# Both halves of an expert tile's first layer issued ahead of the two relus

## The chip, the core and the metric

The kernel runs on one core of one Trainium2 chip. The metric is the device time of one execution in microseconds (us). PE (TensorE) multiplies, DVE (VectorE) and ACT (ScalarE) read its results out of PSUM, POOL (GpSimd) and SP (SyncE) start most of the transfers.

## What is computed

An attention layer with softly sorted key and value blocks makes 3072 tokens of 512 numbers. Each token then goes through one of eight experts, a network of two layers with a relu between them, and is scaled by its gate. The change touches only the expert part:

```python
e_idx = np.argmax(logits, axis=1)
...
for e in range(E):
    mask = e_idx == e
    h = np.maximum(x[mask] @ w1[e], 0.0)
    out[mask] = gate_w[mask, None] * (h @ w2[e])
```

Here `w1[e]` is 512 x 1024 and `w2[e]` is 1024 x 512.

## The kernel before

The attention part writes its tokens, in blocks of 96, into a scratch area in HBM (`xs_scratch`), sorted by expert. Four groups of tokens are placed by `place(m)`: eight scattered writes each, from POOL. The expert part then goes through the scratch area in slots of 128 tokens. The first eleven slots (0 to 10) take tokens of the first three groups, for experts whose tiles are already full; a table `tab1` says which expert and which rows. The slots from 11 on take the rest from `tab2`. In this execution 25 slots ran, 0 to 24.

A slot `s` has these steps:

- `x_load(s)`: SP reads the row number from the table and loads 128 tokens (129 KB) into one of six buffers `xt_b`.
- `mX(s)`: PE transposes the tokens in four pieces (tile `mx`), and DVE copies the result to SBUF (L594).
- `mL1(s)`: PE's sequencer reads the expert's offset from the table (L607). PE multiplies into the PSUM tile `hp`, which has two banks of 512 columns. Four matmuls fill a half. DVE applies the relu to half 0 (L615), ACT to half 1 (L617). Both write `h_b` in `ubuf`.
- `mH(s)`: PE transposes `h` in two groups of four (tile `ht`); DVE copies the first group, ACT the second (L626).
- `mL2(s)`: eight matmuls into `yp`; ACT scales the result (L636); POOL scatters it to the output (L644).

The code is scheduled by hand: each engine runs its instructions in the order in which the program writes them. `run` writes for slot `s`: `mL1(s)`, `mX(s+1)`, `mL2(s-1)`, `x_load(s+5)`, `mH(s)`, with extra jobs (`hooks`) in some slots. On PE a slot is therefore: half 0, half 1, transposes of the next tokens, second layer of the slot before, transposes of `h`. The small PSUM tiles `mx` and `ht` share two buffers, so the second `ht` group of a slot needs DVE's copy of `mx` (L594) of that slot.

The hooks that matter here: slots 0 and 1 finish the gate of the last token group, and `place(3)` scatters it; slots 3, 4 and 5 compute the second table on DVE (`t2_a` with `pad_table`, `t2_b`, `t2_c`), between the relu of half 0 and L594. At the end of slot 5, after `x_load(10)`, SP runs `pad_fill`: eight writes of zero rows into the scratch area (L578), each of which waits for the one before it to land. `x_load(11)` follows on SP and reads the scratch area too.

The tile library keeps track of PSUM by tile: a matmul that writes `hp` waits for every read of `hp` that stands ahead of it in the program, and a read waits for every write ahead of it.

Of the kernel before, what the change touches and what calls it, by code (L numbers as in the profile page):

```python
# [17 lines left out]
def kernel(  # L18
# [561 lines left out]
    def slot_tab(s):  # L580
        return (tab1, s) if s < S1 else (tab2, s - S1)
# [16 lines left out]
    def w_mm(s, *a, **kw):  # L598
        ins = nc.tensor.matmul(*a, **kw).ins  # L599
        if s < S1:  # L600
            for d in w_dma[3]:
                tc.declare_no_dep(ins, d, reason="experts of this slot were loaded before")
            p1_mm.append(ins)

    def mL1(s):
        tb, n = slot_tab(s)
        ev = nc.values_load(tb[0:1, 0, n:n + 1], engines=(PEng,), min_val=0, max_val=(E - 1) * WCOL)  # L607
        hp = scpsum.tile([128, 2, 512], FP32, tag="sc", name=f"hp{s}")
        for half in range(2):
            for c in range(4):  # L610
                w_mm(s, hp[:, half], xT_b[s % 3][:, c],
                     w_all[:, bass.ds(ev + (c * F + half * 512), 512)], start=(c == 0), stop=(c == 3))
            hd = h_b[s % 2][:, half * 512:(half + 1) * 512]
            if half == 0:
                nc.vector.tensor_scalar(hd, hp[:, half], 0.0, None, ALU.max)  # L615
            else:
                nc.scalar.activation(hd, hp[:, half], ACT.Relu)  # L617
        st_["ev", s] = ev
# [102 lines left out]
    def run(sl, pre=()):  # L721
        mX(sl[0])
        for s in sl:
            mL1(s)
            for f, a in hooks.get((s, 0), []):
                f(*a)
            if s + 1 in sl:
                mX(s + 1)
            if s - 1 in sl:
                mL2(s - 1)  # L730
            for f, a in hooks.get((s, 1), []):
                f(*a)
            if s + XB - 1 < SU and s >= 1:
                x_load(s + XB - 1, scat[3] if s + XB - 1 == S1 else ())
            for f, a in hooks.get((s, 2), []):
                f(*a)
            mH(s)
        mL2(sl[-1])
# [6 lines left out]
    for s in range(SU, SMAX):  # L745
        rest.enter_context(tc.If(n2 > s - S1))
        x_load(s)
        mX(s)
        mL1(s)
        mH(s)  # L750
        mL2(s)
# [31 lines left out]
```

## Time and profile before

| | us |
|---|---|
| median of 3 runs | 319.65 |
| lowest and highest | 319.55, 321.23 |
| the profiled execution | 320.09 |
| its span | 318.3 |
| PE busy | 207.5 |
| DVE busy | 152.3 |
| ACT busy | 98.0 |
| POOL busy | 113.3 |

The span is the time between the first and the last instruction in the trace; all positions below count from its start. Busy times are sums over the whole span, of which the attention part takes the first 170 us or so and the slots the rest, so a busy share says little about either part. The list of waits says who stood still for whom; the timeline lists instructions in order of time, and in brackets how long the engine had been idle before and what ended it.

### The profile page before, as it was taken

What the parts mean: (1) busy time and instruction counts of PE and PEld (TensorE: products, weight loads), DVE (VectorE), ACT (ScalarE), POOL (GpSimd) and SP (SyncE); (2) the same over time, 40 slices, a digit from 0 to 9 for tenths busy, and PEclk for the clock granted to TensorE, in tenths of its full rate; (3) what the DMA queues carried; (4) which work ended last, traced back from release to release, by engine and by line L of the source; (5) the groups of instructions that cost most, each with busy time, mean ns of one, the idle gap of its engine ahead of it and who ended that gap; (6) DMA issues with size and microseconds to landing.
All of it is one profiled execution on the core that took longest, in us unless ns stands there. A gap on an engine that the chain in (4) does not pass through costs nothing. (4 is left out here: it accounts for less than half of the span.)

```text
span 318.3 us, 5924 instructions
## 1 busy us (share of the span) xinstructions
PE 207.5 (65%) x1929; PEld 138.9 (44%) x1929; DVE 152.3 (48%) x442; ACT 98.0 (31%) x163; POOL 113.3 (36%) x237
## 2 busy tenths in 40 slices
PE   0017726389998810698733788889898888989840
PEld 0016625278877710586521444444444444444320
DVE  7985548855665630667930355732333233233200
ACT  2004312046555410254300133333333323233320
POOL 8960047304058230380730048420413132231320
PEclk9999999999999999999999999999999999999995
DMA  6999059205112999320212112522342122211110
GB/s 102 221 180 191 4 96 173 32 2 82 20 39 65 171 211 204 54 75 15 65 38 83 35 45 77 164 98 96 122 134 99 55 93 59 93 53 66 63 46 2
DMA packets 21072, 28.05 MB, mean 88 GB/s; under 512 B 5935, under 2 KB 16431, under 8 KB 20784
## 3 DMA queue, kind: packets, MB, share of 16 engines
q0 software_dynamic: 12704, 23.11, 33.5%
q1 hardware_dynamic: 8336, 4.52, 6.1%
q8 instruction: 19, 0.31, 0.4%
q14 instruction: 13, 0.11, 0.1%
HBM read 106.11 MB, written 10.91 MB: 368 GB/s over the span
## 5 line engine op out<-in xcount | busy, mean ns | idle before, releaser
L599 PE MATMUL hp<-w_all,ubuf 128*128 x200 | 52.9, 388 | 21.4 <-DVE ubuf L615 19.6
L599 PEld LDWEIGHTS <-ubuf 128*128 128x128 bf16 x400 | 37.4, 98 | 63.1 <-issue 29.4
L644 POOL DMA_INDIRECT out_dram<-v_sb,ix x25 | 24.7, 990 | 80.3 <-ACT ubuf L626 55.6
L599 PE MATMUL yp<-w_all,ubuf 128*128 x200 | 47.2, 379 | 0.4 <-DVE ubuf L626 0.4
L414 POOL DMA_INDIRECT xs_scratch<-xb,dest x32 | 30.2, 943 | 41.5 <-issue 20.4
L617 ACT ACTIVATE ubuf<-hp 128x512 bf16<-128x512 f32 x25 | 14.9, 597 | 68.1 <-PE hp L599 65.4
L314 ACT ACTIVATE attnT<-sc 96x768 bf16<-96x768 f32 x32 | 25.2, 808 | 17.4 <-PE sc L308 17.4
L329 DVE TENSOR_TENSOR xb<-op,rs 96x256 bf16<-96x256 f32 x64 | 26.9, 421 | 2.2
L626 DVE COPY ubuf<-ht 128x512 bf16<-128x512 bf16 x25 | 10.6, 425 | 34.6 <-PE ht L625 34.6
L636 ACT ACTIVATE v_sb<-yp,v_sb 128x512 f32<-128x512 f32 x25 | 17.2, 688 | 32.1 <-PE yp L599 32.1
L594 DVE COPY ubuf<-mx 128x512 bf16<-128x512 bf16 x25 | 10.6, 423 | 33.7 <-PE mx L593 33.6
L615 DVE TENSOR_SCALAR ubuf<-hp 128x512 bf16<-128x512 f32 x25 | 17.3, 693 | 19.2 <-PE hp L599 19.2
L325 PE MATMUL op<-v_sb,attnT 96*128 96x65 bf16 x256 | 20.7, 245 | 0.1
L213 PEld LDWEIGHTS <-w_all 128*128 128x128 bf16 x192 | 11.5, 129 | 19.3 <-issue 18.7
L221 PE MATMUL va<-bdv,w_all 128*128 128x128 bf16 x128 | 17.1, 306 | 4.1 <-DVE v_sb L223 2.1
L294 PE MATMUL tq<-ident,w_all 128*128 128x128 bf16 x48 | 6.6, 309 | 18.8 <-DVE w_all L128 18.8
L223 ACT CAST v_sb<-va 96x512 bf16<-96x512 f32 x24 | 13.6, 583 | 16.6 <-PE va L221 15.5
L328 DVE RECIPROCAL rs<-op 96x4 f32<-96x4 f32 x64 | 11.0, 172 | 14.2 <-PE op L325 14.1
L325 PEld LDWEIGHTS <-attnT 96*128 96x128 bf16 x256 | 17.4, 134 | 0.6 <-DVE xb L329 0.6
L216 ACT CAST w_all<-ka 128x512 bf16<-128x512 f32 x18 | 10.3, 587 | 23.7 <-PE ka L213 23.6
L221 PEld LDWEIGHTS <-w_all 128*128 128x128 bf16 x128 | 14.2, 181 | 6.3 <-issue 5.8
L593 PE MATMUL mx<-ident,v_sb 128*128 128x128 bf16 x100 | 10.1, 226 | 9.7 <-DMA v_sb<-xs_scratch 9.7
(170 smaller groups left out, 315.4 us busy)
## 6 DMA issues: line engine op xcount, KB each, us to landing
w_all<-in_moe_w_dram POOLq DMA_DIRECT2D x40, 1024.0 KB
v_sb<-xs_scratch SPq DMA_DIRECT2D x25, 129.0 KB, 2.0
v_sb<-in_k_dram POOLq DMA_DIRECT2D x6, 512.0 KB
w_all<-in_v_dram POOLq DMA_DIRECT2D x2, 1536.0 KB
ubuf<-in_q_dram POOLq DMA_DIRECT2D x16, 192.0 KB
xs_scratch<-v_sb SPq DMA_DIRECT2D x9, 129.0 KB, 2.1
xs_scratch<-xb,dest POOLq DMA_INDIRECT x32
out_dram<-v_sb,ix POOLq DMA_INDIRECT x25
```

The lines of the kernel that those rows point to most:

```text
L213: nc.tensor.matmul(acc[:, z], k_il[:, ch * 8 + z].rearrange("p r d -> p (r d)"), bd_k[g], start=True, stop=True)
L221: nc.tensor.matmul(acc[:, z], v_cols[:, ch * 4 + z], bd_v[g], start=True, stop=True)
L223: (nc.scalar.copy if act else nc.vector.tensor_copy)(dst, acc[0:BLK].rearrange("p z x -> p x z"))
L314: nc.scalar.activation(attnT[u % 2][:, 0:8 * BLK].rearrange("p (r f) -> p r f", r=2), sc_tiles.pop(u)[0:BLK, :, 0:4 * BLK], ACT.Exp, scale ...
L325: nc.tensor.matmul(op[:, j], attnT[u % 2][:, c0:c0 + 128], v_sb[g][0:BLK, par * 64 + h * 8 + i, 0:D + 1], start=True, stop=True)
L329: nc.vector.tensor_tensor(xt[:, par * 4:(par + 1) * 4, h * D:(h + 1) * D], op[0:BLK, :, 0:D], rs.broadcast_to([BLK, 4, D]), ALU.mult)
L414: ins = nc.gpsimd.indirect_dma_start(out=xs_dram, out_offset=bass.IndirectOffsetOnAxis(ap=dest[:, t:t + 1], axis=0), in_=xt.bitcast(I32)[: ...
L599: ins = nc.tensor.matmul(*a, **kw).ins
L615: nc.vector.tensor_scalar(hd, hp[:, half], 0.0, None, ALU.max)
L617: nc.scalar.activation(hd, hp[:, half], ACT.Relu)
L636: nc.scalar.activation(y, yp, ACT.Copy, scale=xt.bitcast(FP32)[:, Dm // 2 + 1:Dm // 2 + 2])
L644: ins = nc.gpsimd.indirect_dma_start(out=out, out_offset=bass.IndirectOffsetOnAxis(ap=ix, axis=0), in_=y, in_offset=None, bounds_check=N - ...
```

## The change

The loop over the halves is split. All eight matmuls of the first layer are written first, then the two relus. No instruction is added or removed, and on every engine the instructions stand in the same order as before. What differs is the waits that the library derives.

```diff
             for c in range(4):
                 w_mm(s, hp[:, half], xT_b[s % 3][:, c],
                      w_all[:, bass.ds(ev + (c * F + half * 512), 512)], start=(c == 0), stop=(c == 3))
+        for half in range(2):
             hd = h_b[s % 2][:, half * 512:(half + 1) * 512]
             if half == 0:
                 nc.vector.tensor_scalar(hd, hp[:, half], 0.0, None, ALU.max)
```

On PE, at the border of half 0 and half 1 in one of the later slots, before (the third row is the first matmul of half 1; ISA is a register step of the sequencer; DVE_49 is a semaphore that counts finished DVE instructions):

```order
L599 LDWEIGHTS ubuf
L599 ISA
L599 MATMUL hp_3853<-w_all,ubuf 128x512 [waits DVE_49]
L599 LDWEIGHTS ubuf
L599 ISA
```

and after, the same place:

```order
L599 LDWEIGHTS ubuf
L599 ISA
L599 MATMUL hp_3853<-w_all,ubuf 128x512
L599 LDWEIGHTS ubuf
L599 ISA
```

The wait of the first matmul of half 1 for DVE's relu is gone.

On PE, at the transposes of `h`, before:

```order
L625 LDWEIGHTS ubuf
L625 MATMUL ht_0_3831<-ident,ubuf 128x128 [waits PE_49]
...
L625 LDWEIGHTS ubuf [waits Activation_49]
L625 MATMUL ht_1_3837<-ident,ubuf 128x128 [waits DVE_49]
...
L607 TENSOR_LOAD tab_463
L607 ISA x2
L599 LDWEIGHTS ubuf
```

and after (lines behind the change count one higher):

```order
L626 LDWEIGHTS ubuf [waits DVE_49]
L626 MATMUL ht_0_3831<-ident,ubuf 128x128 [waits PE_49]
...
L626 LDWEIGHTS ubuf [waits Activation_49]
L626 MATMUL ht_1_3837<-ident,ubuf 128x128 [waits DVE_49]
...
L607 TENSOR_LOAD tab_463
L607 ISA x2
L599 LDWEIGHTS ubuf
```

The first transpose now waits itself for DVE's relu of half 0; the wait of the second group for ACT's relu stood there before, and the sequencer's table read for the next slot still stands behind it.

On ACT, the three instructions of a slot, before:

```order
L617 ACTIVATE ubuf<-hp_2967 128x512 [waits DVE_49,PE_49,Activation_49]
L636 ACTIVATE v_sb_73<-yp_2984,v_sb_73 128x512 [waits DMAHW7_49,DMASW2_49,PE_49]
L626 COPY ubuf<-ht_1_3116 128x512 [waits PE_49,Activation_49]
L617 ACTIVATE ubuf<-hp_3132 128x512 [waits DVE_49,PE_49,Activation_49]
L636 ACTIVATE v_sb_73<-yp_3149,v_sb_73 128x512 [waits DMAHW0_49,DMASW3_49,PE_49]
```

and after:

```order
L618 ACTIVATE ubuf<-hp_2967 128x512 [waits DVE_49,Activation_49]
L637 ACTIVATE v_sb_73<-yp_2984,v_sb_73 128x512 [waits DMAHW7_49,DMASW2_49,PE_49]
L627 COPY ubuf<-ht_1_3116 128x512 [waits PE_49,Activation_49]
L618 ACTIVATE ubuf<-hp_3132 128x512 [waits DVE_49,Activation_49]
L637 ACTIVATE v_sb_73<-yp_3149,v_sb_73 128x512 [waits DMAHW0_49,DMASW3_49,PE_49]
```

The relu of half 1 waits for DVE's relu of half 0 in both kernels. Before, it waited for PE beside it; after, DVE's relu itself waits for all eight matmuls, and its end covers PE's.

## Rows read from the trace of the kernel before

**Rows 1.** The page, chain that ended last: shares of the span by engine.

```profile
PE 34%; DVE 7%; DMA 1%; issue 1%; POOL 0%; ACT 0%; POOLq 0%; SPq 0%
```

**Rows 2.** List of waits, slots alone: total us, times, longest us.

```profile
PE hp L599 <- DVE ubuf L615: 19.6, 25, 0.8
```

**Rows 3.** Timeline, one late slot: start us, us, engine, line, instruction, count, idle before.

```profile
253.41 1.03 PE L599 MATMUL hp<-w_all,ubuf 128*128 x4
254.47 0.69 DVE L615 TENSOR_SCALAR ubuf<-hp 128x512 bf16<-128x512 f32 x1 [0.66 <-PE hp L599]
255.22 1.02 PE L599 MATMUL hp<-w_all,ubuf 128*128 x4 [0.78 <-DVE ubuf L615]
256.08 0.39 PE L593 MATMUL mx<-ident,v_sb 128*128 128x128 bf16 x4
256.30 1.89 PE L599 MATMUL yp<-w_all,ubuf 128*128 x8
256.33 0.60 ACT L617 ACTIVATE ubuf<-hp 128x512 bf16<-128x512 f32 x1 [2.00 <-PE hp L599]
256.50 0.42 DVE L594 COPY ubuf<-mx 128x512 bf16<-128x512 bf16 x1 [1.34 <-PE mx L593]
258.03 0.61 PE L625 MATMUL ht<-ident,ubuf 128*128 128x128 bf16 x8
258.48 1.03 PE L599 MATMUL hp<-w_all,ubuf 128*128 x4
```

**Rows 4.** Timeline, slots 3 to 5: slot 3's start, relus, copies, layers.

```profile
191.68 1.03 PE L599 MATMUL hp<-w_all,ubuf 128*128 x4
...
192.74 0.69 DVE L615 TENSOR_SCALAR ubuf<-hp 128x512 bf16<-128x512 f32 x1 [0.66 <-PE hp L599]
...
194.81 0.40 DVE L594 COPY ubuf<-mx 128x512 bf16<-128x512 bf16 x1
...
197.81 0.69 DVE L615 TENSOR_SCALAR ubuf<-hp 128x512 bf16<-128x512 f32 x1 [0.66 <-PE hp L599]
...
201.50 0.42 DVE L594 COPY ubuf<-mx 128x512 bf16<-128x512 bf16 x1
...
202.75 1.02 PE L599 MATMUL hp<-w_all,ubuf 128*128 x4 [0.40 <-issue]
...
203.81 0.69 DVE L615 TENSOR_SCALAR ubuf<-hp 128x512 bf16<-128x512 f32 x1 [1.56 <-PE hp L599]
...
205.64 1.89 PE L599 MATMUL yp<-w_all,ubuf 128*128 x8
...
206.45 0.42 DVE L594 COPY ubuf<-mx 128x512 bf16<-128x512 bf16 x1
...
207.56 0.69 ACT L636 ACTIVATE v_sb<-yp,v_sb 128x512 f32<-128x512 f32 x1 [1.30 <-PE yp L599]
```

**Rows 5.** Timeline, SP's issues: load 10, first zero write, load 11; PE's transposes for 11.

```profile
208.38 0.33 SPq L586 DMA_DIRECT2D v_sb<-xs_scratch  x1
...
210.64 0.35 SPq L578 DMA_DIRECT2D xs_scratch<-v_sb  x1
...
228.39 0.35 SPq L586 DMA_DIRECT2D v_sb<-xs_scratch  x1
...
230.75 0.39 PE L593 MATMUL mx<-ident,v_sb 128*128 128x128 bf16 x4
```

**Rows 6.** Line L586, all token loads: us from issue to landing.

```profile
DMA to landing us min/median/max: 1.9/2.0/2.7
```

**Rows 7.** Stretches behind the last matmul: busy PE, PEld, DVE, ACT, POOL; granted clock.

```profile
306.30:309.30 3.00, 0.00 (x0) 0.00 (x0) 0.00 (x0) 0.69 (x1) 1.18 (x2) 1.00 0.27 93
309.50:312.00 2.50, 0.00 (x0) 0.00 (x0) 0.00 (x0) 0.00 (x0) 0.00 (x0) 0.50 0.06 16
```

**Rows 8.** Timeline, slot 0: half 0 after a long idle time.

```profile
173.17 1.87 PE L599 MATMUL hp<-w_all,ubuf 128*128 x4 [0.83 <-DVE ubuf L594]
```

## The prediction

> **What bounds the kernel now.** I read the chain that ended last first. In it PE holds the largest share and DVE the next [rows 1], so the slots, where PE works without pause, set the end. The list of waits for the slots comes next: PE waits for DVE's relu at every one of the 25 slots, 19.6 us in total [rows 2]. The timeline of a late slot shows how [rows 3]. Half 0 starts at 253.41, DVE's relu runs from 254.47 to 255.16, and half 1 starts at 255.22 after 0.78 us without a matmul. Nothing else in that slot holds PE. ACT's relu, DVE's copy of the transposed tokens and ACT's scaling all lie beside the second layer's eight matmuls.
>
> The idle time understates the wait. From start to start, half 0 takes 1.81 us (253.41 to 255.22) and half 1, four equal matmuls with work right behind them, takes 0.86 (255.22 to 256.08) [rows 3]. The gap is worth 1.81 - 0.86 = 0.95 us, since the last matmul of half 0 also has to drain before the relu may start.
>
> **The change in a regular slot.** The starts of PE's steps give the slot's sum [rows 3]: half 0 1.81, half 1 0.86, token transposes 0.22, second layer 1.73, transposes of h 0.45, together 5.07. Without the wait half 0 takes 0.86 too, so the slot takes 4.12. The gain is 0.95.
>
> What moves later has to fit into 4.12. DVE's relu starts 1.06 us after the start of the half that it waits for [rows 3]; that is now half 1, so it runs from 0.86 + 1.06 = 1.92 to 2.61 us of the slot. ACT's relu waits for DVE's, not only for PE, so it follows with its 0.60 us and ends near 3.25. The transposes of h, which read both, are due at 0.86 + 0.86 + 0.22 + 1.73 = 3.67. That is 0.4 us of cover. DVE's copy of the tokens [rows 3] now comes behind the relu, from about 2.55 to 2.97, which is earlier than ACT's end.
>
> One more step is queued behind the transposes: PE's sequencer reads the next slot's table entry only when the second group has been released. What that costs shows at the end of slot 4, where the second group waits for the copy that ends at 201.92 and the next half 0 starts at 202.75, 0.83 later, with 0.40 of idle time put down to issue [rows 4]. So the next slot can start no earlier than 3.25 + 0.83 = 4.08, and is due at 4.12. The cover just holds. If DVE's or ACT's release came 0.3 us later than I read, each slot would take 4.4; below zero it cannot go, as 4.12 is PE's own work. I take 4.12.
>
> **Slots 3 to 5.** Here DVE computes the second table behind its relu, and the later relu pushes this work back. The distances from the relu's start to the start of the token copy (L594) are 2.07, 3.69 and 2.64 us [rows 4], and they stay, as DVE is serial there. A slot in which the copy is late then takes 1.92 + distance + 0.42 + 0.83: 5.24, 6.86 and 5.81 us. That is about as long as before or longer; slot 4 took 1.06 + 3.69 + 0.42 + 0.83 = 6.00. So these slots gain nothing and slots 4 and 5 lose some.
>
> Slot 3 started at 191.68 [rows 4]. Three gaps lie ahead of it, 2.85 us. I take off 0.2, an estimate by the same working, since in slot 1 DVE's placement of the last tokens starts after the later relu. Slot 3 then starts at 189.03, slot 4 at 194.27, slot 5 at 201.13, slot 6 at 206.94. In slot 5 the second layer of slot 4 starts after two halves and the transposes, at 201.13 + 1.94 = 203.07, where it was 205.64 [rows 4]: 2.57 earlier.
>
> **What is late next.** ACT's scaling at 207.56 [rows 4] frees the buffer for load 10, which SP issues at 208.38; then come eight zero writes, one after another, from 210.64; then load 11 at 228.39 [rows 5]. This chain takes 228.39 - 210.64 = 17.75 us, and nothing in the change shortens it. It moves with ACT's scaling, by 2.57, so load 11 is issued at 225.82. Tokens land 2.0 us later [rows 6]; with about 0.15 for PE to start, an estimate, the transposes for slot 11 start at 228.0. Before, they started at 230.75 [rows 5], when the tokens had just landed (228.39 + 2.0 = 230.4) and PE did not have to wait.
>
> PE alone would be there sooner: slot 6 at 206.94, four slots of 4.12 to slot 10 at 223.42, and 1.72 more for its two halves, 225.1. So PE stands still for some 2.8 us. Up to that point the kernel gains 230.75 - 228.0 = 2.75 us, though eleven gaps (10.5 us) were removed.
>
> **The sum.** Behind it lie the gaps of slots 11 to 24, 14 x 0.95 = 13.3. Together 2.75 + 13.3 = 16.05. Loads 12 and later come much faster than slots, and POOL's 1 us per scatter fits. What follows the last matmul depends on it as before. Against the profiled execution, 320.09, the sum gives 304.04. The median of the three runs is 0.44 lower, so I predict 319.65 - 16.05 = 303.6 for the median. Own range of this case: the chain of zero writes at 2.0 us each (the median landing of a load) would take 16.0 instead of 17.75, at 2.4 each 19.2, so the gain ahead of slot 11 lies between 4.5 and 1.3: 301.9 to 305.1.
>
> **Rivals.**
>
> *The chain of zero writes is not in the way.* If its steps shorten, or SP gets there sooner, PE sets the pace: 225.1 instead of 228.0 for slot 11, a gain of 5.65 + 13.3 = 18.95, time 300.7. Against it speaks that load 11 landed only 0.35 us ahead of its use before.
>
> *ACT's relu becomes the bound.* The cover worked out above is 0.04 us. With 0.3 us more per slot on the path DVE, ACT, transposes, table read, each gap is worth 0.65: 2.75 + 14 x 0.65 = 11.85, time 307.8. For it speaks the serial pair of relus; against it, that I used durations of the trace for each link.
>
> *TensorE's clock falls in the idle time ahead of slot 11.* [...] In slot 0, after a long idle time, four matmuls took 1.87 us [rows 8] where later ones take 1.03 [rows 3]; in slot 3 they are at 1.03 again [rows 4]. If some 7 us after the idle time ran at that level, half of it, 3.5 us, would be lost: 307.1.
> [...] The trace's end agrees with the fall; no run here shows yet what 2.8 us inside does. [...]
>
> *Slower than before.* The same fall, but without return: PE's work per slot would go from 4.12 to about 1.87 / 1.03 of it, 7.5 us, and 14 slots would add 47 us to the sum. Every us of work that runs at the lower level costs nearly one more, so it decides from about 16 us of work on. [...]
>
> *The change does nothing.* Then the wait of half 1 would have to stay; the derived waits say it is gone.
>
> **How the numbers follow.** A measurement of this kernel tells about 0.5% (1.6 us) from no change. Forecast: 0.67. Chain not in the way: 0.09, 300.7. ACT's relu: 0.10, 307.8. Clock: 0.10, 307.1. Slower: 0.02. Nothing: 0.02. The first four are all faster by over 0.5%, 0.96. The range takes the forecast's own, 301.9 to 305.1, and reaches to the rivals on both sides as far as half of their chance: 300.9 to 307.3.
>
> **What would show it.** In the trace after: PE's wait for DVE's relu is gone from the list; half 0 and half 1 run as eight matmuls; DVE's relu starts 1.06 us after half 1 starts, and ACT's right after DVE's; late slots are 4.12 us apart; slots 3 to 5 take about 5.2, 6.9 and 5.8; load 11 is issued near 225.8 and PE waits 2 to 3 us for it ahead of slot 11. I am wrong if late slots are more than 4.2 apart (cover), if PE does not wait for load 11 (chain), if matmuls behind that wait take about 1.9 us for four (clock), or if the zero writes' chain has changed its length.

## The result, and the profile after

| us | before | after |
|---|---|---|
| median | 320.44 (4 runs) | 307.68 (4 runs) |
| lowest and highest | 319.55, 321.59 | 306.60, 309.65 |
| the profiled execution | 320.09 | 309.65 |
| its span | 318.3 | 307.5 |

Three of the four times of before are those given further up. The ratio of after to before is 0.961, with a 95% interval of 0.954 to 0.967. Ratios, here and below, are formed from the undisturbed executions alone and are not the quotients of the medians, which take all of them; the two differ by up to 0.005. The kernel is faster, as forecast, but by 12.8 us instead of 16.05. The forecast was 303.6, and the measured 307.68 lies just above the range that was given (300.9 to 307.3). The profiled execution is the longest of the four, 5.6 us above the 304.04 that the forecast had for it.

In the page of after, the chain that ended last has lost most of DVE's share and gained some of DMA's, against [rows 1]:

```profile
PE 29%; DMA 7%; DVE 3%; issue 1%; ACT 0%; POOL 0%; POOLq 0%; SPq 0%
```

The list of waits of after for the slots (engine, line, what it waited for: total us, times, longest us) answers to [rows 2]. PE's 25 waits for DVE's relu are gone. What PE waits for now is tokens (two waits, 9.3 us ahead of slot 0, where before had 9.7, and 4.4 us ahead of slot 11) and DVE's copy. "Issue" is idle time for which the trace shows no releaser; at a slot's start PE's sequencer reads the table in it, for 0.298 to 0.572 us, 0.302 in the median of 25 reads.

```profile
ACT ubuf L618 <- DVE ubuf L616: 60.5, 23, 17.7
...
PE mx L593 <- DMA v_sb<-xs_scratch: 13.7, 2, 9.3
...
PE hp L599 <- issue: 2.4, 5, 0.8
PE ht L626 <- DVE ubuf L594: 2.4, 2, 2.0
```

A late slot in the timeline of after (start us, us, engine, line, instruction, count, idle before and its end), against [rows 3]:

```profile
247.55 1.89 PE L599 MATMUL hp<-w_all,ubuf 128*128 x8
...
249.48 0.69 DVE L616 TENSOR_SCALAR ubuf<-hp 128x512 bf16<-128x512 f32 x1 [1.55 <-PE hp L599]
249.50 1.89 PE L599 MATMUL yp<-w_all,ubuf 128*128 x8
...
250.08 0.41 DVE L594 COPY ubuf<-mx 128x512 bf16<-128x512 bf16 x1
250.26 0.60 ACT L618 ACTIVATE ubuf<-hp 128x512 bf16<-128x512 f32 x1 [1.82 <-DVE ubuf L616]
...
251.22 0.61 PE L626 MATMUL ht<-ident,ubuf 128*128 128x128 bf16 x8
...
251.70 1.89 PE L599 MATMUL hp<-w_all,ubuf 128*128 x8
```

The two halves are one run of eight matmuls. The next slot starts 251.70 - 247.55 = 4.15 us later, where it was 5.07. DVE's relu starts 1.93 us into the slot, the copy follows it, ACT's relu ends at 250.86, and the transposes of `h` start at 251.22 without a wait on PE. Slots 12 to 24 all look like this, 4.14 to 4.19 us apart.

So the late slots did what was forecast. The rest is in the stretches between the marks that the prediction used (us; the start of the transposes for slot 0, load 10 and load 11 as SP issues them, the transposes for slot 11, the start of slot 12, the last matmul of the second layer):

| stretch | before | after | change | forecast |
|---|---|---|---|---|
| start to transposes for slot 0 | 171.73 | 170.43 | -1.30 | 0 |
| to load 10 | 36.64 | 36.23 | -0.41 | -2.57 |
| load 10 to load 11 | 20.02 | 21.01 | +0.99 | 0 |
| to the transposes for slot 11 | 2.36 | 2.24 | -0.12 | -0.18 |
| to slot 12 | 7.46 | 9.35 | +1.89 | -0.95 |
| slots 12 to 24 | 67.69 | 55.83 | -11.86 | -12.35 |
| behind them | 12.40 | 12.40 | 0.00 | 0 |

The first row is attention, which the change doesn't touch. From slot 0 on after gains 9.5 us of the forecast 16.05. Of the missing 6.5 us, 3.2 are ahead of slot 11 (2.16 up to load 10, 0.99 in the zero writes, 0.06 behind them), 2.84 in the stretch from there to slot 12, and 0.49 in the late slots.

Slots 3 to 6 in the timeline of after, PE with one row of ACT, against [rows 4]:

```profile
187.60 1.89 PE L599 MATMUL hp<-w_all,ubuf 128*128 x8
...
193.15 1.89 PE L599 MATMUL hp<-w_all,ubuf 128*128 x8 [0.75 <-issue]
...
199.25 0.38 PE L626 MATMUL ht<-ident,ubuf 128*128 128x128 bf16 x4 [2.03 <-DVE ubuf L594]
200.30 2.60 PE L599 MATMUL hp<-w_all,ubuf 128*128 x8 [0.67 <-issue]
...
203.12 2.70 PE L599 MATMUL yp<-w_all,ubuf 128*128 x8
...
205.85 0.69 ACT L637 ACTIVATE v_sb<-yp,v_sb 128x512 f32<-128x512 f32 x1 [1.53 <-PE yp L599]
...
206.83 1.89 PE L599 MATMUL hp<-w_all,ubuf 128*128 x8 [0.40 <-issue]
```

Slots 3, 4 and 5 take 5.55, 7.15 and 6.53 us (187.60 to 193.15 to 200.30 to 206.83), not 5.24, 6.86 and 5.81. In slot 5 the same eight matmuls last 2.60 and 2.70 us where they lasted 1.89. The reason is in the windows (busy PE, PEld, DVE, ACT, POOL; then the granted clock):

```profile
177.50:201.30 23.80, 19.36 (x139) 10.49 (x137) 12.26 (x50) 8.21 (x14) 13.79 (x24) 1.00 0.27 86
201.40:204.70 3.30, 3.30 (x12) 1.48 (x11) 1.63 (x6) 0.60 (x1) 0.00 (x0) 0.50 0.34 100
...
228.70:235.40 6.70, 5.49 (x22) 2.77 (x23) 0.85 (x2) 1.21 (x2) 0.38 (x2) 0.50 0.44 120
```

Between 177.5 and 300.3 us the clock twice stood at 0.50: for 3.3 us shortly behind the idle time in slot 4 (2.03 us, four transposes, 0.67 us), and for 6.7 us from within the idle time ahead of slot 11. Before had neither, its granted clock was 1.00 from 179.7 to 309.4. The granted clock alone does not give the pace: in after it stood at 0.50 from 70 to 177 us too, and the matmuls of L325 and L342 between 100 and 165 took 0.244 and 0.278 us on average, as in before at 1.00. In the two stretches here the matmuls themselves are longer. The second stretch in the timeline of PE, after:

```profile
223.63 1.89 PE L599 MATMUL hp<-w_all,ubuf 128*128 x8
229.91 0.61 PE L593 MATMUL mx<-ident,v_sb 128*128 128x128 bf16 x4 [4.40 <-DMA v_sb<-xs_scratch]
230.31 3.62 PE L599 MATMUL yp<-w_all,ubuf 128*128 x8
...
234.58 2.33 PE L599 MATMUL hp<-w_all,ubuf 128*128 x8
...
239.26 1.89 PE L599 MATMUL hp<-w_all,ubuf 128*128 x8
```

and SP's issues of after (load 10, first zero write, load 11), against [rows 5]:

```profile
206.66 0.33 SPq L586 DMA_DIRECT2D v_sb<-xs_scratch  x1
208.87 0.36 SPq L578 DMA_DIRECT2D xs_scratch<-v_sb  x1
...
227.67 0.35 SPq L586 DMA_DIRECT2D v_sb<-xs_scratch  x1
```

Load 11 leaves at 227.67, 0.72 earlier than before; as attention had given 1.30, it leaves 0.58 later against slot 0. PE has finished slot 10's two halves at 225.5, 5.4 earlier than before. The eight zero writes took 227.67 - 208.87 = 18.80 us, where they took 17.75.

### The profile page after: what moved, and what is told of

It reads as the page before. It is cut to its first block, busy times and chain, and to the rows that moved or that the text cites. A ratio compares the mean times of both kernels' runs of the same rounds, so it can differ in the third digit from the quotient of the medians.

```text
span 307.5 us, 5922 instructions
## 1 busy us (share of the span) xinstructions
PE 208.3 (68%) x1929; PEld 140.3 (46%) x1929; DVE 150.0 (49%) x442; ACT 98.3 (32%) x163; POOL 113.5 (37%) x237
## 5 line engine op out<-in xcount | busy, mean ns | idle before, releaser
L599 PEld LDWEIGHTS <-ubuf 128*128 128x128 bf16 x400 | 39.1, 101 | 43.2 <-issue 7.9
L599 PE MATMUL hp<-w_all,ubuf 128*128 x200 | 50.0, 395 | 3.3 <-issue 2.4
L599 PE MATMUL yp<-w_all,ubuf 128*128 x200 | 49.8, 394 | 0.4 <-DVE ubuf L627 0.4
L325 PE MATMUL op<-v_sb,attnT 96*128 96x65 bf16 x256 | 20.5, 243 | 0.1
L213 PEld LDWEIGHTS <-w_all 128*128 128x128 bf16 x192 | 11.1, 126 | 19.6 <-issue 19.1
L626 PE MATMUL ht<-ident,ubuf 128*128 128x128 bf16 x200 | 16.7, 226 | 2.6 <-DVE ubuf L594 2.4
L626 PEld LDWEIGHTS <-ubuf 128*128 128x128 bf16 x200 | 14.1, 101 | 9.0 <-issue 3.6
L325 PEld LDWEIGHTS <-attnT 96*128 96x128 bf16 x256 | 17.2, 133 | 0.6 <-DVE xb L329 0.6
```

Of the source, the lines that this page charges most:

```text
L325: nc.tensor.matmul(op[:, j], attnT[u % 2][:, c0:c0 + 128], v_sb[g][0:BLK, par * 64 + h * 8 + i, 0:D + 1], start=True, stop=True)
L626: nc.tensor.transpose(tp[:, c], h_b[s % 2][:, fc * 128:(fc + 1) * 128], ident)
```

## The experiments

The theory was: (a) in the late slots the change gains what was forecast; (b) what it gains ahead of slot 11 is swallowed by the zero writes; (c) the idle time that this leaves lowers the clock. The rivals were that the early slots themselves lose by the later relu, and that the serial pair of relus limits every slot.

The runs lie on three chips: e1 to e4, e5 to e8 and e9 to e11. Ratios are to the kernel before on the same chip, and medians are compared on one chip alone.

| kernel | median us | before there | ratio, 95% |
|---|---|---|---|
| e1_again | 319.55 | 330.90 | 0.963 (0.956 to 0.971) |
| e2_late_only | 318.93 | 330.90 | 0.962 (0.953 to 0.972) |
| e3_pad_free | 312.88 | 330.90 | 0.942 (0.935 to 0.950) |
| e4_warm | 317.78 | 330.90 | 0.957 (0.949 to 0.964) |
| e5_early_only | 322.10 | 321.34 | 0.998 (0.993 to 1.002) |
| e6_two_banks | 308.04 | 321.34 | 0.958 (0.953 to 0.962) |
| e7_two_banks_pad | 299.77 | 321.34 | 0.933 (0.929 to 0.937) |
| e8_before_pad | 320.25 | 321.34 | 0.997 (0.994 to 1.001) |
| e9_after | 308.43 | 322.53 | 0.959 (0.951 to 0.968) |
| e10_warm_both | 307.01 | 322.53 | 0.950 (0.942 to 0.958) |
| e11_relu_free | 309.93 | 322.53 | 0.960 (0.953 to 0.967) |

The stretches of the profiled executions, with the marks of the table above (e5 and e8 are compared by their times):

| kernel | to load 10 | load 10 to 11 | to transposes 11 | to slot 12 | slots 12 to 24 |
|---|---|---|---|---|---|
| e1_again | 41.05 | 22.37 | 2.56 | 8.41 | 55.82 |
| e2_late_only | 43.69 | 20.53 | 2.90 | 6.55 | 55.94 |
| e3_pad_free | 40.41 | 14.15 | 5.37 | 7.97 | 55.87 |
| e4_warm | 40.87 | 21.35 | 2.57 | 6.65 | 55.93 |
| e6_two_banks | 34.04 | 21.12 | 2.76 | 8.63 | 55.43 |
| e7_two_banks_pad | 33.31 | 14.06 | 3.59 | 6.52 | 55.43 |
| e9_after | 36.00 | 21.83 | 2.19 | 8.23 | 55.88 |
| e10_warm_both | 34.56 | 21.55 | 2.64 | 6.65 | 55.93 |
| e11_relu_free | 36.27 | 21.16 | 2.83 | 8.21 | 55.43 |

### e1: the changed kernel again

No edit; it is there to be compared with the next three on the same chip.

> The changed kernel once more, beside the others. All theories: about 307.7 us (ratio to before 0.960). The chain theory says that PE stands still for 3 to 5 us ahead of the token transposes of slot 11, behind load 11, and that the four matmuls behind it are near 1.9 us and not near 1.0; if matmuls there are at full speed in this execution, the time is 2 to 3 us shorter than in the profiled execution (309.65).

The ratio repeated (0.963 against 0.961); the time did not, as the kernel before, too, takes about 10 us more on this chip. Here DVE and ACT stood still for 2.6 and 5.1 us in slot 4, with a releaser that the trace gives only as "remote" (last section), so the first stretch is 4 to 5 us longer than elsewhere. Slot 11 in the timeline of PE, e1:

```profile
240.93 0.61 PE L593 MATMUL mx<-ident,v_sb 128*128 128x128 bf16 x4 [5.85 <-DMA v_sb<-xs_scratch]
241.33 3.48 PE L599 MATMUL yp<-w_all,ubuf 128*128 x8
```

PE waits 5.85 us for load 11, somewhat more than expected, and the second layer's eight matmuls behind the wait take 3.48 us in place of 1.89, as expected.

### e2: the change in the late slots alone

```diff
 (S1 is 11; relu(half) holds the two relus' lines)
+        both = s >= S1
         for half in range(2):
             for c in range(4):
                 w_mm(...)
+            if not both:
+                relu(half)
+        if both:
+            relu(0)
+            relu(1)
```

> The change in slots 11 to 24 alone; slots 0 to 10 as before. Theory A (the chain of zero writes swallows the gain of the early slots, and the idle time costs clock): 14 gaps of 0.92 us are gained, no wait for load 11, no lower clock: 320.4 - 12.9 = 307.5 us, the same as the whole change, within 1 us. Theory B (the early slots gained something real, the late ones are worth less than 0.92): slower than the whole change by 2 us or more, 309.5 and up.

The time is that of the whole change: 318.93 against 319.55 for e1, ratios 0.962 and 0.963. The change in the early slots is worth nothing that can be told, though there too a regular slot is about 0.9 us shorter with it. The timeline of PE of e2 shows the way to slot 11 without it:

```profile
241.82 0.40 PE L593 MATMUL mx<-ident,v_sb 128*128 128x128 bf16 x4 [0.85 <-DMA v_sb<-xs_scratch]
242.06 1.89 PE L599 MATMUL yp<-w_all,ubuf 128*128 x8
```

With the longer slots PE waits 0.85 us instead of 5.85, the clock stays at 1.00 there, and the second layer takes 1.89. Up to load 10 e1 is 2.6 us ahead of e2 (41.05 against 43.69), of which about 1.1 is a different length of the stall in slot 4 (10.74 against 11.84 us for the slot). The zero writes take back 1.8 of it (20.53 to 22.37) and the stretch to slot 12 1.9 (6.55 to 8.41).

### e3: the zero writes without their chain

```diff
 (in pad_fill, behind each of the eight zero writes)
+            tc.declare_no_dep(ins.ins, group="zeros", reason="each expert has its own rows")
+            tc.add_to_no_dep_group("zeros", ins.ins)
```

> The whole change, and the eight zero writes no longer wait for each other (each expert has its own rows). Theory A: the chain from the first zero write to load 11 shrinks from 18.8 us to about 10 to 12, PE does not wait ahead of slot 11, the clock stays there: 4.4 us of idle time and some 2.8 us of slow work are saved, 307.7 - 7 = 300.5 us. Theory B (the early slots are held up by DVE's table work alone, and PE would be late anyway): 1 us or less is saved, 306.5 to 307.7.

This takes 6.7 us off the changed kernel (319.55 to 312.88). From the first zero write to load 11 it is 11.94 us instead of 20.06, from load 10 to load 11 14.15 instead of 22.37, and PE does not wait for load 11 any more:

```profile
234.76 0.39 PE L595 MATMUL mx<-ident,v_sb 128*128 128x128 bf16 x4
234.98 1.89 PE L601 MATMUL yp<-w_all,ubuf 128*128 x8
```

That was the transposes for slot 11 in the timeline of PE of e3: no idle time in front of them, no slow matmul behind them. The 5.37 us behind load 11 are not PE's wait: the tokens lay there before PE came. Slots 10 and 11 take 4.85 us each, with 0.57 and 0.38 of issue, so the stretch to slot 12 is 7.97.

### e4: matmuls in the idle time ahead of slot 11

```diff
 (in run, behind mL1(s))
+            if s == 10:
+                dummy = opsum.tile([128, Dm], FP32, tag="op", name="dummy")
+                for _ in range(18):
+                    nc.tensor.matmul(dummy, ident, xT_b[s % 3].rearrange("p c r -> p (c r)"), start=True, stop=True)
```

> The whole change, and 18 matmuls of 512 columns that nobody reads behind slot 10's first layer (18 x 0.215 = 3.9 us), in the time in which PE waits for load 11. Theory A with the clock as a cost of its own: PE's waiting time is filled, load 11 comes as late as before, but slot 11's matmuls run at full speed: 307.7 - 2.5 = 305.2 us. If the slow matmuls behind the wait had another cause than the idle time, the same 307.7 us, with four matmuls near 1.9 us there as before.

Eighteen matmuls that nobody reads, 4.05 us, fill the wait. In the timeline of PE of e4:

```profile
237.00 4.05 PE L731 MATMUL dummy<-ubuf,ident 128*128 128x512 bf16 x18
241.43 0.40 PE L593 MATMUL mx<-ident,v_sb 128*128 128x128 bf16 x4 [0.38 <-DMA v_sb<-xs_scratch]
241.66 1.89 PE L599 MATMUL yp<-w_all,ubuf 128*128 x8
```

The clock stays at 1.00 there, and the stretch to slot 12 takes 6.65 us instead of 8.41 (e1). More work made it 1.8 us shorter, where 2.5 was expected. That is the price of the lower clock in slot 11, as this stretch begins behind the wait. The median fell by 1.8 too (319.55 to 317.78), and each of e4's four times lies below each of e1's.

### e5: the change in the early slots alone

```diff
+        both = s < S1
```

> The change in slots 0 to 10 alone; slots 11 to 24 as before. Theory A (chain and clock): load 11 is issued about as late as before, PE waits for it, and one or two slots behind it run at the lower clock: ratio to before 1.00 to 1.01. Theory B (the early slots gain what the prediction gave them, 2.75 us): ratio 0.992.

No difference that can be told (0.993 to 1.002); the 0.992 of theory B lies outside, if narrowly. The trace has the wait ahead of slot 11 (3.94 us) and the clock at 0.50 behind it (229.3 to 236.1). With e2 this says it from the other side: early slots gain nothing that can be told, late ones the rest.

### e6: the order of before, with the two banks declared independent

```diff
             for c in range(4):
-                w_mm(...)
+                mm = w_mm(...)
+                if half == 1:
+                    tc.declare_no_dep(mm, relu0, reason="the halves lie in different banks")
             if half == 0:
-                nc.vector.tensor_scalar(hd, hp[:, half], 0.0, None, ALU.max)
+                relu0 = nc.vector.tensor_scalar(hd, hp[:, half], 0.0, None, ALU.max).ins
             else:
-                nc.scalar.activation(hd, hp[:, half], ACT.Relu)
+                r1 = nc.scalar.activation(hd, hp[:, half], ACT.Relu).ins
+                tc.declare_no_dep(r1, relu0, reason="the halves lie in different banks")
```

> The code of before, told that the two halves of hp lie in different banks: half 1 no longer waits for DVE's relu of half 0, that relu still starts behind half 0, and ACT's relu no longer waits for DVE's. PE's gap is gone without pushing DVE's table work back. Theory A: late slots 4.12 to 4.15 us; slots 3 to 5 about 4.4, 6.0 and 5.0; no lower clock in slots 4 and 5 unless the chip's own stall in slot 4 brings it; load 10 and load 11 are issued 1.5 to 2.5 us earlier against slot 0 than with the whole change; PE still waits for load 11. Ratio to before 0.955 (1.5 to 3 us less than the whole change). If the later relu cost nothing: same as the whole change, 0.963.

Here DVE's relu starts behind half 0, beside half 1's matmuls, and ACT's relu waits for PE alone. Late slots are 4.12 us apart (49.48 from the start of slot 12 to that of slot 24). Slots 3 to 5 take 4.83, 6.35 and 5.80 us instead of 5.55, 7.15 and 6.53 in after, so the later relu had pushed DVE's table work back; they were expected at 4.4, 6.0 and 5.0, without a fall of the clock. Load 10 leaves 2.0 us and load 11 2.1 us earlier against slot 0 than in after (36.23 + 21.01 - 34.04 - 21.12 = 2.08), as expected: this gain the zero writes let through. PE then waits 6.06 us for load 11. The total does not tell whether the gain is there: the interval of the ratio, 0.953 to 0.962, holds the expected 0.955 and the 0.961 of the changed kernel. In the timeline of PE of e6 the eight matmuls behind slot 4's idle time take 3.20 us instead of 1.89, as the clock falls here too (0.7 in the page's slice from 198.7 to 206.3):

```profile
197.97 0.38 PE L629 MATMUL ht<-ident,ubuf 128*128 128x128 bf16 x4 [1.23 <-DVE ubuf L594]
199.03 3.20 PE L599 MATMUL hp<-w_all,ubuf 128*128 x8 [0.68 <-issue]
```

### e7: e6 with the zero writes of e3

The edits of e6 and e3 together.

> The same, and the zero writes no longer wait for each other. Theory A: PE waits neither for load 11 nor much in slots 3 to 5; ratio to before about 0.935, faster than the free zero writes with the whole change (0.942) by about 2 us, as its early relu is worth something only when the chain is out of the way. Theory B: same as with the whole change, 0.942.

The best kernel of the study, 299.77 us, ratio 0.933. It is faster than e6 (308.04 on the same chip); against e3, on another chip, the intervals of the ratios just touch, so that difference is not told. PE has no wait ahead of slot 11, and its clock stands at 1.00 from 179.1 to 288.3. Slots 3 to 5 and the transposes for slot 11 in the timeline of PE of e7:

```profile
198.94 0.38 PE L631 MATMUL ht<-ident,ubuf 128*128 128x128 bf16 x4 [1.16 <-DVE ubuf L596]
199.72 1.89 PE L601 MATMUL hp<-w_all,ubuf 128*128 x8 [0.41 <-issue]
...
204.68 1.89 PE L601 MATMUL hp<-w_all,ubuf 128*128 x8 [0.41 <-issue]
...
221.17 1.89 PE L601 MATMUL hp<-w_all,ubuf 128*128 x8
222.89 0.39 PE L595 MATMUL mx<-ident,v_sb 128*128 128x128 bf16 x4
```

Slots 6 to 9 take 4.12 us each ((221.17 - 204.68) / 4).

### e8: the kernel before with the zero writes of e3

> The kernel before, with zero writes that no longer wait for each other. Both theories: the chain of zero writes was hidden before (load 11 landed just ahead of its use), so no change beyond 1 us, ratio 0.997 to 1.0. If it is faster by more, the chain bounded the kernel before already, and the change did not lay it bare.

Ratio 0.997 (0.994 to 1.001): without shorter slots the chain of zero writes costs next to nothing. It is a limit only once the change has made PE quicker. Apart, e8 is worth about 1 us, which can't be told from none, and e6 13; together, in e7, 21.6.

### e9: the changed kernel on the third chip

No edit, the partner of e10 and e11.

> The whole change once more, as the partner of the next two on the same chip: ratio 0.960 to 0.963; late slots 4.15 us apart.

Both falls of the clock are there again (198.9 to 202.3 and 229.6 to 233.0), and slots 12 to 24 are 4.15 us apart or a little more; the first fall, in the windows of e9:

```profile
199.00:202.20 3.20, 3.20 (x12) 1.24 (x11) 0.11 (x1) 0.00 (x0) 0.07 (x1) 0.50 0.55 167
```

### e10: matmuls in both idle times

```diff
 (e4's edit, and in mH, between the two groups of transposes)
+            if z and s == 4:
+                dummy = opsum.tile([128, Dm], FP32, tag="op", name="dummy4")
+                for _ in range(9):
+                    nc.tensor.matmul(dummy, ident, xT_b[s % 3].rearrange("p c r -> p (c r)"), start=True, stop=True)
```

> The whole change with unread matmuls in both places where PE stands still: nine (1.9 us) between the two groups of transposes in slot 4, where PE waits for DVE's table work, and 18 ahead of slot 11. Clock theory: the granted clock stays at 1.00 through slots 5 and 11; slot 5's matmuls run at full speed, so load 10 is issued about 1.5 us earlier against slot 0, and the slots behind load 11 save about 2 us: 3 to 4 us less than the whole change, ratio about 0.950. If PE's idle time were not the cause of the lower clock: the same as the whole change.

The clock stays at 1.00 throughout, as the window from 179.5 to 298.7 of e10 shows, and slot 5 runs at full pace behind the nine unread matmuls (timeline of PE):

```profile
179.50:298.70 119.20, 109.52 (x722) 58.33 (x720) 42.61 (x119) 44.00 (x75) 42.04 (x95) 1.00 0.28 91
```

```profile
198.54 2.10 PE L626 MATMUL dummy<-ubuf,ident 128*128 128x512 bf16 x9
...
201.79 1.89 PE L599 MATMUL hp<-w_all,ubuf 128*128 x8 [0.67 <-issue]
```

Against e9 the stretch to load 10 is 1.44 us shorter (36.00 to 34.56) and that from the transposes for slot 11 to slot 12 1.58 (8.23 to 6.65). The median fell by only 1.4 us, and the intervals of e9 and e10 overlap: the total is not told apart, also because attention took 2.9 us longer in the profiled execution of e10 (171.92 against 169.03). The expected 3 to 4 us are seen in the two stretches alone, 3.0 us together, in one execution of each kernel.

### e11: the changed kernel, ACT's relu not waiting for DVE's

```diff
-                nc.scalar.activation(hd, hp[:, half], ACT.Relu)
+                r1 = nc.scalar.activation(hd, hp[:, half], ACT.Relu).ins
+                tc.declare_no_dep(r1, relu0, reason="the halves lie in different banks")
```

> The whole change, but ACT's relu of half 1 no longer waits for DVE's relu of half 0. If the serial pair of relus makes the late slots 4.15 instead of 4.12 us (it releases the transposes, behind which the sequencer reads the next slot's table entry), they are 4.12 us apart now: 14 x 0.03 = 0.4 us, too little for the time to show. If DVE's copy of the tokens or the table read alone set the 4.15, they stay at 4.15.

The timeline of e11, a late slot:

```profile
260.62 1.89 PE L599 MATMUL hp<-w_all,ubuf 128*128 x8
...
262.55 0.69 DVE L616 TENSOR_SCALAR ubuf<-hp 128x512 bf16<-128x512 f32 x1 [1.52 <-PE hp L599]
262.61 0.60 ACT L618 ACTIVATE ubuf<-hp 128x512 bf16<-128x512 f32 x1 [1.07 <-PE hp L599]
...
264.75 1.89 PE L599 MATMUL hp<-w_all,ubuf 128*128 x8
```

Both relus run side by side, DVE's from 262.55 to 263.24 and ACT's from 262.61 to 263.21, each as long as in after, where one follows the other (0.69 and 0.60 us), and the slot takes 264.75 - 260.62 = 4.13 us (4.12 on average). So the serial pair costs 0.03 us a slot, 0.4 us in all.

## Why the prediction was off, step by step

**The late slots: right.** The gap was worth 0.912 us each, not 0.95 (67.69 - 55.83 over 13 slots). The serial chain of DVE's relu, ACT's relu, transposes and table read, for which the prediction had 0.04 us of cover, is a little over it: 4.15 in place of 4.12, and e11, where it is cut, has 4.12. The rival of ACT's relu was the right mechanism at a tenth of its size.

**What is late next: the right mechanism, the term of 2.75 us mis-sized.** Two steps of the sum failed: this gain ahead of slot 11 (2.75 us forecast, 0.46 lost), and the lower clock behind load 11, which the sum put at nothing and which cost 2.70 in the profiled execution. That the zero writes would hold load 11, and that eleven removed gaps would vanish behind them, is what e2 (early slots add nothing), e5 (nothing alone), e3 (6.7 us once the chain is cut) and e8 (nothing without the change) show. But the term had load 10 leave 2.57 us earlier and got 0.41, and took the chain at its old length and got 0.99 more. Up to the transposes for slot 11 nothing was gained at all (36.64 + 20.02 + 2.36 = 59.02 before, 36.23 + 21.01 + 2.24 = 59.48 after). The 2.16 us up to load 10 can be read from the timeline of slots 3 to 6 above:

- The clock fell behind slot 4's idle time, to 0.50 from 201.4 to 204.7. The second layer starts 203.12 - 200.30 = 2.82 us into slot 5 instead of 1.94, and ACT's scaling 205.85 - 203.12 = 2.73 us behind it instead of 207.56 - 205.64 = 1.92 [rows 4]: 0.88 + 0.81 = 1.69 us. The prediction's own numbers had slot 4 at 6.86 us with 4.12 us of work for PE, so this idle time could have been read from them, but it weighed the clock at slot 11 only. In e10, where the clock stays up, the stretch is 1.44 us shorter than in e9, though its slots 3 and 4 are 0.21 us longer each.
- The table read behind the copy took longer. The prediction used one row, 0.83 us from the copy's end to the next matmul, with 0.40 put down to issue [rows 4]. In after, issue is 0.75 and 0.67 us at the end of slots 3 and 4, and 0.40 only at the end of slot 5. Slots 3 and 4 are 0.31 and 0.29 us longer than forecast, 0.60 together. The read itself accounts for 0.20 and 0.27 of it.

The table reads (L607; count, shortest, median and longest in ns, start in us) at the end of slot 4 of before, and of slots 3 and 4 of after:

```profile
L607 PEldq TENSOR_LOAD <-tab x1: 299/299/299, 202.0 to 202.0; - x1
...
L607 PEldq TENSOR_LOAD <-tab x1: 496/496/496, 192.0 to 192.0; - x1
...
L607 PEldq TENSOR_LOAD <-tab x1: 572/572/572, 199.3 to 199.3; - x1
```

What makes the read take the one or the other time is open; at the end of slot 5 of after, where issue is 0.40, it took 0.299.

Slots 0 to 2 came out 0.12 us better than forecast, and 1.69 + 0.60 - 0.12 = 2.17.

The chain's added 0.99 us is open. With the writes still chained, it was longer in all kernels with shorter early slots (20.8 to 22.4 us from load 10 to load 11) than in e2 (20.5) and before (20.0). The writes then run beside other work than before; whether any of it slows them was not tried.

**The rival of the clock: it came true, as an addition and not as a case apart.** The wait ahead of slot 11 was foreseen at 2.8 us and measured 4.40: against slot 0, load 11 came 3.15 us later than forecast and PE only 1.6. The clock stood at 0.50 from 228.6 to 235.5, and the stretch to slot 12 took 9.35 us, where e4 and e10, at 1.00, take 6.65: 2.7 us in the profiled run, and 1.6 to 1.8 between two kernels of one chip (e9 and e10, e1 and e4). The rival's chance of 0.10 was low: before has a fall at its end, some 3 us behind the last matmul [rows 7], and after and every experiment with an unfilled wait of 3.9 us or more here (e1 5.85, e5 3.94, e6 6.06, e9 4.3, e11 4.6 us) show one. That the rival's 307.1 came within 0.6 us of the measured time is in part luck: it has one fall at 3.5 us, and the run had two, with a longer chain of zero writes beside them. No run shows the rival's term, 3.5 us lost in 7 us at half pace: the second fall of after lasted 6.9 us, 1.3 of them without a matmul, and cost 2.70. Slot 0 of before, from which the pace was read [rows 8], shows no lower clock either, as 1.00 is granted there from 165 to 181 us, through the wait of 9.7 us ahead of it too; what slowed its matmuls is open. The first fall of after came in slot 5, behind 2.03 + 0.67 us of idle time in slot 4. Shorter idle times left the clock at 1.00: 0.78 us in every slot of before, and 1.16 + 0.41 us in e7.

**Sum.** Of the missing 6.5 us the clock has 1.69 + 2.70 = 4.39 in the profiled execution, the zero writes 0.99, the late slots 0.49, slots 3 and 4 less the better start 0.60 - 0.12; what is left is 0.06 behind load 11 and 0.14 in slot 11. This execution is the longest of the four, 2.0 us above the median. The other three have no trace, so which of the parts is smaller in them was not seen. Two of the prediction's own signs of being wrong came: the matmuls behind the wait at half pace, and a chain of zero writes of another length. Of the other rivals none came: PE did wait for load 11, the waits for the relu did go, and nothing got slower. One reading of the prediction was wrong without harm: ACT's scaling starts at 258.23, behind the second layer's matmuls of [rows 3] and not beside them.

## What to carry to other kernels

Where a removed stall puts an engine ahead of a transfer, walk the transfer's chain before counting the gain: here eleven of 25 removed gaps were worth nothing that can be told until the zero writes ran side by side, and that edit alone was worth nothing that can be told either. Where the forecast itself leaves TensorE idle inside a busy stretch about as long as here (2.03 + 0.67 us in slot 4, 4.40 us ahead of slot 11), put the lower clock, which took 1.69 and 2.70 us here, into the sum, not beside it. And the two-bank PSUM tile, which the library tracks as one, cost time here in either order (5.07 and 4.15 us for the late slots shown of before and after, 4.12 in e6): with the banks declared independent, the old order has the short slots too, and its relus stay early.

## What was not expected of the hardware

- TensorE's clock fell after 1.23 + 0.68 us of idle time, with four transposes between the two, in e6 (0.7 in the page's slice, 3.20 us for the next eight matmuls) and after 2.03 + 0.67 us in after (2.60 us, granted clock 0.50); in e7, after 1.16 + 0.41 us, it did not (1.89 us, 1.00). With nine unread matmuls in that place (2.10 us, e10) it stayed at 1.00.
- Work nobody needs made the kernel no slower (317.78 us, e1 319.55) and its slot 11 quicker: 4.05 us of it in e4 for 1.8 us off the stretch.
- On the chip of e1 to e4 DVE and ACT stood still for 1.8 to 5.1 us at a time in slot 4, with a releaser that the trace gives only as "remote", by no engine's name, in the changed slot of e1 and the unchanged one of e2, and the kernel before took 330.9 us there against 320 to 323 on the others. The row of ACT in slot 4 of e1 (timeline, idle time before in brackets):

```profile
203.92 0.58 ACT L627 COPY ubuf<-ht 128x512 bf16<-128x512 bf16 x1 [5.06 <-remote]
```

The cause is open.
